# A mixer kernel on one core: the state products of the attention as two 64-column tiles a head

## The chip, the cores and the metric

One core of a Trainium2 chip runs the whole program. The metric is the device time of one execution in microseconds (us), median of three runs. A profile is one execution recorded by the hardware profiler. TensorE (PE, with PEld for its weight loads), VectorE (DVE), ScalarE (ACT), GpSimd (POOL) and SyncE (SP, which here issues DMAs) each run their own list of instructions in order, and semaphores tie the lists together.

## The reference

```
# attention, B,H,S,D = 4,8,768,48
for t in range(S):                      # complex decay a, normalised to |a| <= 0.999
    new_re = ar * S_re - ai * S_im
    new_im = ar * S_im + ai * S_re
    S_re   = new_re + k[t] (outer) v[t]
    y[t]   = q[t] @ S_re
x = y as (B, S, H*D)                    # 4 x 768 x 384
# first MLP block
u = x + ((x^T @ U @ V)^T)               # rank 32 over the sequence
x = u + relu(u @ w1) @ w2               # 384 -> 1536 -> 384
# second MLP block
u = x + real(fft(fft(x, axis=1), axis=2))
x = u + relu(layernorm(u) @ w1') @ w2'
```

## The kernel before

The attention is computed in chunks of 128 time steps: 4 batches of 6 chunks. For each chunk, a chain of DVE, ACT and POOL operations (`decays`, `turns`) turns the decays into factors and multiplies them into queries and keys. The result is `QK` (time on the free axis, 128 partitions); SP copies it by six DMAs to `QT` (96 partitions: 48 real and 48 imaginary parts; 8 heads). Then `products` (written as a generator; one `yield` a step) does on PE:

- `scores` (L501): for each head, keys times queries, 128 x 128, into `sc`; DVE masks it into `pm` (L506).
- `turned` (L511): six transposes of the keys into `kp`; ACT copies them (L513) into `ks`, a tile of 128 time steps x 768 columns, 96 columns a head.
- `summed` for `y` (L522): for each head, `pm` times `v` and, from the second chunk on, `QT` times the state `S`. The stationary operand has 128 columns (time), taken as two tiles of 64 columns (`halves`), which write PSUM partitions 0 to 63 and 64 to 127.
- `summed` for `g` (L522): for each head, `ks` times `v`, which gives what the chunk adds to the state. The stationary operand has 96 columns, taken as a tile of 64 columns and one of 32: the slice is cut at the end of the head.
- DVE then makes the new state `S` of 96 x 384 from `g` (L570, or L572 and L573). There is a `g` in all chunks but the last of a batch: 5 x 4 = 20 state products.

`ks` comes from the pool slots tagged `st` (three of them). The same slots stage the MLP weights, which come in as 64-bit words (`fetch`, L127, tiles `stw`), are turned to f32 by ACT and DVE (L120, L142, L143: `wxw`) and split into a high and a low 16-bit part by ACT (L164) and POOL (L165, L166: `w`). There are 24 such pieces a layer. `check_w` (L176) reads the weights once and writes an unread tile `chk`.

The first MLP's units (`moe_units`) run 12 hidden blocks for each half batch: nine matmuls `hp` of 128 x 384 (L103 to L105), ACT and DVE make `hh` and `hl` from them (L230, L231), and nine matmuls into `acc` (L212, L213, L198). The attention of batch b+1 and, at the end, the Fourier transform of batch 0 are put in beside the units of batch b as side work, some steps a unit. The first batch's attention runs alone, before the first MLP starts (60 to 125 us). The second MLP has the Fourier transforms beside it.

The code gives each step a priority; a list scheduler, run at build time with its own timing of each engine, writes the instruction order of each engine. A change of a few instructions can so move others.

Of the kernel before, what the change touches and what calls it, by code (L numbers as in the profile page):

```python
# [9 lines left out]
BF16 = mybir.dt.bfloat16  # L10
F32 = mybir.dt.float32
F32R = mybir.dt.float32r
I32 = mybir.dt.int32
# [9 lines left out]
DM = H * D  # L23
# [23 lines left out]
def mixer_kernel(ctx, tc, a_in, qk_in, v_in, u_in, v4_in, w_in, cc_in, ss_in, cb_in, sb_in, id_in, mask_in, rows_in, out):  # L47
    nc = tc.nc
    V, A, G, T = nc.vector, nc.scalar, nc.gpsimd, nc.tensor
# [3 lines left out]
    moe = ctx.enter_context(tc.tile_pool(name="moe", bufs=2))  # L53
# [8 lines left out]
    def bank(name, pool=None):  # L62
        pool = pool or pms
        return pool.tile([128, 512], F32, tag={id(pms): "ms", id(pacc): "acc", id(phid): "hid"}[id(pool)], name=name)
# [58 lines left out]

    def fetch(src, name):
        n = src.shape[-1]
        st = moe.tile([128, 384, 2], I32, tag="st", name=f"st{name}", bufs=3)[:, :n]
        nc.sync.dma_start(st.rearrange("p n w -> p (n w)"), src.bitcast(I32))  # L127
        return st

# [41 lines left out]
    def check_w(mi, f, z):  # L171

        hi = wt[mi, f][:, 0, z * 384 : (z + 1) * 384]
        unread = ft(f"chk{mi}_{f}_{z}", [128, 384], BF16, tag="chk", bufs=2)
        at = stats[:, list(BOUNDS).index(("w1", "w2")[z]), mi * FB + f : mi * FB + f + 1]
        V.scalar_tensor_tensor(out=unread, in0=hi, scalar=1.0, in1=hi, op0=ALU.mult, op1=ALU.mult, accum_out=at)  # L176

# [74 lines left out]
    def stat(name, b, c):  # L252
        return stats[:, list(BOUNDS).index(name), b * NC + c : b * NC + c + 1]
# [8 lines left out]
    def attention_pool():  # L262
        pl = attp[0]

        def at(nm, tag=None, bufs=4, shape=(128, 3, 2, 128), dt=F32, pl=pl):
            return pl.tile(list(shape), dt, tag=tag or "t", name=nm, bufs=bufs)

        return at
# [22 lines left out]
    def load_v(b, c):  # L291
        if c == NC:
            b, c = b + 1, 0
        if 0 < b < B:
            t = attention_pool()(f"vin{b}_{c}", "vin", 2, (128, DM))
            nc.sync.dma_start(t, v_in[b, c])
            inp["v", b, c] = t
# [182 lines left out]
    def products(m, j):  # L480

        b, cc = PAIRS[m]
        c = cc[j]
        n = f"{b}_{c}"
        last = c == NC - 1
        at = attention_pool()

        def t3(nm, bufs, shape):
            return at(f"{nm}{n}", nm, bufs, shape)

        QT, QK = qkt[b, c]
        vin = inp["v", b, c]
        sc, pm, kp = [], [], []
        pool = pacc if b == 0 else pms
        halves = slice(0, 64), slice(64, 128)

        def scores(hf):
            ps = bank(f"sc{n}_{hf}").rearrange("p (h t) -> p h t", h=4)
            for h in range(4):
                q = QT[:, hf * 4 + h]  # L500
                T.matmul(ps[:, h, :], q[:, 128:256], q[:, :128], start=True, stop=True)  # L501
            sc.append(ps)

        def masked(hf):
            pm.append(room[:, hf] if b == 0 else at(f"pm{n}_{hf}", "pm", 2, (128, 4, 128)))
            V.tensor_tensor(pm[hf], sc[hf], mask.unsqueeze(1).to_broadcast([128, 4, 128]), ALU.mult)  # L506

        def turned(z):
            kp.append(bank(f"kp{n}_{z}", pool)[:, :384])
            for i in range(3):  # L510
                T.transpose(kp[z][:, i * 128 : (i + 1) * 128], QK[:, z, i, 128:256], ident)  # L511
            src = kp[z].rearrange("t (x h) -> t h x", h=8)
            A.copy(ks.rearrange("t (h z x) -> t h z x", h=8, z=2)[:, :, z, :], src)  # L513

        def summed(out, ops):

            for o, (l, r) in enumerate(ops):
                for h in range(8):
                    hsl = slice(h * 48, (h + 1) * 48)
                    for p in halves:  # L520
                        p = slice(p.start, min(p.stop, l(h).shape[-1]))
                        T.matmul(  # L522
                            out[p, hsl],
                            l(h)[:, p],
                            r[:, hsl],
                            start=h == 0 and o == 0,
                            stop=h == 7 and o == len(ops) - 1,
                            skip_group_check=True,
                        )

        if b == 0:
            if len(rooms) < 4:
                rooms.append(wpl.tile([128, 3, 4, 128], F32, tag="w", name=f"pm{n}"))
            room = rooms[c % 4]
        scores(0)
        scored.append(nc.cur_bb.bb.instructions[-1])
        yield
        scores(1)
        masked(0)
        yield  # L540
        masked(1)
        if not last:
            ks = moe.tile([128, 768], F32, tag="st", name=f"k{n}", bufs=3)
            turned(0)
        yield
        if not last:
            turned(1)
            fe = t3("fe", 2, (96, 8))
            G.tensor_scalar(fe, QT[:, :, 256], 1.0 / FSCALE, 0.0, ALU.mult, ALU.add)
        load_v(b, c + 1)  # L550
        yield
        S = state.get(b)
        yp = bank(f"y{n}", pool)[:, :DM]
        ops = [(lambda h: pm[h // 4][:, h % 4], vin)]
        if S is not None:
            ops.append((lambda h: QT[:, h, :128], S))
        summed(yp, ops)
        yield
        if not last:
            gp = bank(f"g{n}")[:96, :DM]  # L560
            summed(gp, [(lambda h: ks[:, h * 96 : (h + 1) * 96], vin)])
        x = xt[b, c] = xpl[0].tile([128, DM], F32, tag="x", name=f"x{n}", bufs=10)
        A.activation(x, yp, AF.Copy, scale=1.0 / FSCALE)
        yield
        if not last:
            state[b] = sS = t3("S", 2, (96, DM))
            by_head = lambda o: o.rearrange("p (h e) -> p h e", h=8)
            f3 = fe.unsqueeze(2).to_broadcast([96, 8, 48])
            if S is None:
                V.scalar_tensor_tensor(out=by_head(sS), in0=by_head(gp), scalar=FSCALE, in1=f3, op0=ALU.mult, op1=ALU.mult)  # L570
            else:
                V.scalar_tensor_tensor(out=sS, in0=gp, scalar=FSCALE, in1=S, op0=ALU.mult, op1=ALU.add)  # L572
                V.tensor_tensor(by_head(sS), by_head(sS), f3, ALU.mult)  # L573
        yield
        A.activation(yp, x, AF.Square, accum_out=stat("y", b, c))
# [130 lines left out]
    def both(m):  # L706
        return urgent(chain(products(m, 0), products(m, 1)), 250)
# [82 lines left out]
    def ft(name, shape, dt=F32, tag=None, bufs=1):  # L790
        return pfl[0].tile(list(shape), dt, tag=tag or name.split(".")[0], name=name.replace(".", "_"), bufs=bufs)
# [446 lines left out]
```

## Time and profile before

| | us |
|---|---|
| median of 3 runs (lowest, highest) | 987.97 (986.28, 989.13) |
| the profiled execution, its own time | 987.67 |
| its span from first to last instruction | 985.4 |
| PE busy | 865.6 (88%) |
| DVE busy | 612.9 (62%) |
| ACT busy | 410.1 (42%) |
| POOL busy | 243.2 (25%) |

Up to 60 us the inputs come in and PE hardly works. From 60 to 118 us PE does the attention of batch 0, from 165 to 510 us the first MLP with the attention of batches 1 to 3 beside it, from 510 to 600 us the first MLP's last batch with the first Fourier transform and the second layer's weights beside it, and from there to the end the second MLP. A matmul on f32 data stands in the trace as two records, so a product of 16 matmuls has 32 records.

### The profile page before, as it was taken

Reading aid. Unit: us, or ns where it says so; the run is one execution under the profiler, and the core shown is the slowest. Engines: PE = TensorE matmul, PEld = TensorE weight load, DVE = VectorE, ACT = ScalarE, POOL = GpSimd, SP = SyncE. Lnnn points to the kernel's source line nnn. Section 1 sums busy time; section 2 is a strip of 40 time slices with the busy share of each in tenths; the row PEclk is TensorE's granted clock in tenths of the full one; section 3 lists DMA queues with packets and bytes.
Section 4 is the critical chain, followed back from the end, with each engine's and each line's share of the span. In section 5 each row is a group of like instructions: output and inputs, shape, how many; then the busy total and the mean of one; then the engine's idle time right before and its main releaser. Section 6 shows DMA issues by size and latency. Waiting matters only on the chain. (4 is left out here: it accounts for less than half of the span.)

```text
span 985.4 us, 16779 instructions
## 1 busy us (share of the span) xinstructions
PE 865.6 (88%) x6686; PEld 585.0 (59%) x6686; DVE 612.9 (62%) x1116; ACT 410.1 (42%) x767; POOL 243.2 (25%) x271
## 2 busy tenths in 40 slices
PE   0059985799999999999996889999999999999997
PEld 0047843477667676667763455666666765766664
DVE  7976895966776565473389995672645564463221
ACT  8545675667666754542333341122122211322111
POOL 3402453430112012020066551320322232020000
PEclk9999997799999998989999999999999999999999
DMA  9069648557546743514175240110101021000000
GB/s 363 1 83 143 180 129 159 119 100 145 100 121 101 132 105 73 105 34 74 51 228 187 82 121 1 41 41 1 65 18 49 1 81 49 1 25 10 17 25 27
DMA packets 47095, 83.43 MB, mean 85 GB/s; under 512 B 5600, under 2 KB 36064, under 8 KB 47008
## 3 DMA queue, kind: packets, MB, share of 16 engines
q1 hardware_dynamic: 45152, 75.96, 33.3%
q0 software_dynamic: 1856, 6.31, 1.8%
q8 instruction: 54, 0.88, 0.4%
q14 instruction: 33, 0.27, 0.1%
HBM read 53.79 MB, written 9.44 MB: 64 GB/s over the span
## 5 line engine op out<-in xcount | busy, mean ns | idle before, releaser
L231 DVE SCALAR_TENSOR_TENSOR hl<-hp,hh 128x384 f16<-128x384 f32 x192 | 105.6, 551 | 190.9 <-ACT hh L230 190.1
L230 ACT ACTIVATE hh<-hp 128x384 f16<-128x384 f32 x192 | 93.4, 487 | 299.6 <-PE hp L105 285.3
L212 PE MATMUL acc<-w,hh 128*128 128x384 f16 x576 | 190.4, 332 | 8.5 <-ACT hh L230 7.7
L213 PE MATMUL acc<-w,hh 128*128 128x384 f16 x576 | 189.6, 330 | 1.4 <-POOL w L166 1.4
L198 PE MATMUL acc<-w,hl 128*128 128x384 f16 x576 | 127.7, 330 | 0.0
L103 PE MATMUL hp<-u,w 128*128 128x384 f16 x288 | 95.8, 334 | 19.9 <-DVE hl L231 18.8
L105 PE MATMUL hp<-u,w 128*128 128x384 f16 x288 | 96.9, 336 | 3.8 <-POOL w L166 3.8
L104 PE MATMUL hp<-u,w 128*128 128x384 f16 x288 | 96.3, 334 | 1.0 <-DVE u L640 1.0
L103 PE MATMUL hp<-n,w 128*128 128x384 f16 x288 | 93.9, 326 | 1.0 <-DVE hl L231 1.0
L104 PE MATMUL hp<-n,w 128*128 128x384 f16 x288 | 93.9, 326 | 0.0
L105 PE MATMUL hp<-n,w 128*128 128x384 f16 x288 | 93.9, 326 | 0.0
L104 PEld LDWEIGHTS <-w 128*128 128x128 f16 x576 | 56.9, 99 | 60.4 <-issue 26.6
L212 PEld LDWEIGHTS <-hh 128*128 128x128 f16 x576 | 56.9, 99 | 47.8 <-ACT hh L230 11.3
L105 PEld LDWEIGHTS <-w 128*128 128x128 f16 x576 | 56.9, 99 | 43.5 <-POOL w L166 4.2
L198 PEld LDWEIGHTS <-hl 128*128 128x128 f16 x576 | 56.6, 99 | 39.0 <-issue 1.8
L103 PEld LDWEIGHTS <-w 128*128 128x128 f16 x576 | 56.8, 99 | 37.9 <-issue 1.6
L501 PE MATMUL sc<-QT 96*128 96x128 f32 x384 | 59.5, 305 | 20.8 <-DMA QT<-QK 20.5
L213 PEld LDWEIGHTS <-hh 128*128 128x128 f16 x576 | 57.2, 99 | 34.2 <-issue 3.4
L522 PE MATMUL g<-vin,k 128*32 128x48 f32 (+1 forms) x640 | 75.5, 229 | 1.1 <-ACT k L513 1.1
L501 PEld LDWEIGHTS sc<-QT 96*128 96x128 f32 x384 | 53.6, 213 | 24.9 <-issue 20.0
L511 PE MATMUL kp<-ident,QK 128*128 128x128 f32 x120 | 21.0, 297 | 50.5 <-DVE QK L472 50.3
L522 PEld LDWEIGHTS g<-vin,k 128*32 128x32 f32 (+1 forms) x640 | 53.4, 123 | 19.8 <-issue 1.5
(264 smaller groups left out, 1569.3 us busy)
## 6 DMA issues: line engine op xcount, KB each, us to landing
QT<-QK SPq DMA_DIRECT2D x144, 129.0 KB
stw<-in_w_dram SPq DMA_DIRECT2D x48, 384.0 KB
ain<-in_a_dram SPq DMA_DIRECT2D x12, 768.0 KB
qkin<-in_qk_dram SPq DMA_DIRECT2D x12, 768.0 KB
x1d<-x SPq DMA_DIRECT2D x24, 192.0 KB
vin<-in_v_dram SPq DMA_DIRECT2D x18, 192.0 KB
lo<-x1d SPq DMA_DIRECT2D x12, 192.0 KB
out_dram<-lo SPq DMA_DIRECT2D x12, 192.0 KB
```

The source lines that it names most:

```text
L103: T.matmul(o, ah, bh, start=start, stop=False, skip_group_check=skip)
L104: T.matmul(o, ah, bl, start=False, stop=False, skip_group_check=skip)
L105: T.matmul(o, al, bh, start=False, stop=stop, skip_group_check=skip)
L198: T.matmul(acc[t], hl[:, t * 128 : (t + 1) * 128], w2h, start=False, stop=f == FB - 1 and extra is None)
L212: T.matmul(acc[t], hh[:, ts], w2h, start=f == 0, stop=False)
L213: T.matmul(acc[t], hh[:, ts], w2l, start=False, stop=False)
L230: A.activation(hh, hp, AF.Relu)
L231: V.scalar_tensor_tensor(out=hl, in0=hp, scalar=0.0, in1=whole_of(hh), op0=ALU.max, op1=ALU.subtract)
L501: T.matmul(ps[:, h, :], q[:, 128:256], q[:, :128], start=True, stop=True)
L511: T.transpose(kp[z][:, i * 128 : (i + 1) * 128], QK[:, z, i, 128:256], ident)
L522: T.matmul(out[p, hsl], l(h)[:, p], r[:, hsl], start=h == 0 and o == 0, stop=h == 7 and o == len(ops) - 1, skip_group_check=True,)
```

## The change

The keys' tile has 800 columns instead of 768, the last 32 filled with zeros by POOL. Each head's stationary operand for the state product is 128 columns wide, of which the last 32 are the next head's keys (or the zeros), taken as two tiles of 64 columns. The rows 96 to 127 of the product are not read. The slots `st` grow from 3072 to 3200 bytes a partition, and `chk` has one buffer instead of two.

```diff
     def fetch(src, name):
-        st = moe.tile([128, 384, 2], I32, tag="st", name=f"st{name}", bufs=3)[:, :n]
+        st = moe.tile([128, 400, 2], I32, tag="st", name=f"st{name}", bufs=3)[:, :n]
...
     def check_w(mi, f, z):
-        unread = ft(f"chk{mi}_{f}_{z}", [128, 384], BF16, tag="chk", bufs=2)
+        unread = ft(f"chk{mi}_{f}_{z}", [128, 384], BF16, tag="chk", bufs=1)
...
         def turned(z):
-            A.copy(ks.rearrange("t (h z x) -> t h z x", h=8, z=2)[:, :, z, :], src)
+            A.copy(ks[:, :768].rearrange("t (h z x) -> t h z x", h=8, z=2)[:, :, z, :], src)
         def summed(out, ops):
                     for p in halves:
-                        p = slice(p.start, min(p.stop, l(h).shape[-1]))
                         T.matmul(
...
-            ks = moe.tile([128, 768], F32, tag="st", name=f"k{n}", bufs=3)
+            ks = moe.tile([128, 800], F32, tag="st", name=f"k{n}", bufs=3)
+            G.memset(ks[:, 768:], 0.0)
...
-            gp = bank(f"g{n}")[:96, :DM]
-            summed(gp, [(lambda h: ks[:, h * 96 : (h + 1) * 96], vin)])
+            gp = bank(f"g{n}")[:, :DM]
+            summed(gp, [(lambda h: ks[:, h * 96 : h * 96 + 128], vin)])
+            gp = gp[:96]
```

On PE, at the first state product of the program (`g_0` of batch 0; `sc_1` are the next chunk's scores), the order before is:

```order
L501 MATMUL sc_1_1_346<-QT_1_246 128x128 x4
L522 MATMUL g_0_402<-vin_0_126,k_0_305 64x48
L522 MATMUL g_0_402<-vin_0_126,k_0_305 32x48
L522 MATMUL g_0_402<-vin_0_126,k_0_305 64x48
L522 MATMUL g_0_402<-vin_0_126,k_0_305 32x48
L522 MATMUL g_0_402<-vin_0_126,k_0_305 64x48
```

and after the change, where L522 has become L521 and the lines from L562 on are numbered one higher:

```order
L501 MATMUL sc_1_1_347<-QT_1_246 128x128 x4
L521 MATMUL g_0_404<-vin_0_126,k_0_305 64x48 x16
L603 MATMUL z_434<-x_0_421,ust 128x384
L511 MATMUL kp_2_0_484<-ident,QK_2_319 128x128 x3
L511 MATMUL kp_2_1_489<-ident,QK_2_319 128x128 x3
```

The sixteen matmuls that alternated between 64 and 32 rows of output are sixteen of 64. Counted over the whole program's order, the output width changes from one PE matmul to the next 428 times before (306 of them between 64 and 32) and 110 times after (none between 64 and 32).

On DVE, at the end of the attention of batch 3, around the last state (`S_4`) and the first pieces of the second layer's weights (`stw`, `wxw`; `hl` belongs to the first MLP of batch 2), the order before is:

```order
L231 SCALAR_TENSOR_TENSOR hl_2_0_11_4403<-hp_2_0_11_4350,hh_2_0_11_4402 128x384
L120 TENSOR_SCALAR stw_0_1_5055<-stw_0_1_5055 128x384
L143 SCALAR_TENSOR_TENSOR wxw_0_0_5000<-stw_0_0_4998,wxw_0_0_5000 128x384
L640 SCALAR_TENSOR_TENSOR u_1_2_4398<-xp_1_2_4393,u_1_2_4398 128x384
L142 SCALAR_TENSOR_TENSOR wxw_0_1_5057<-wxw_0_1_5057,stw_0_1_5055 128x384
L143 SCALAR_TENSOR_TENSOR wxw_0_1_5057<-stw_0_1_5055,wxw_0_1_5057 128x384
L572 SCALAR_TENSOR_TENSOR S_4_4711<-g_4_4688,S_3_4557 96x384
```

and after:

```order
L143 SCALAR_TENSOR_TENSOR wxw_3_0_5300<-stw_3_0_5298,wxw_3_0_5300 128x384
L120 TENSOR_SCALAR stw_3_1_5350<-stw_3_1_5350 128x384
L142 SCALAR_TENSOR_TENSOR wxw_3_1_5352<-wxw_3_1_5352,stw_3_1_5350 128x384
L143 SCALAR_TENSOR_TENSOR wxw_3_1_5352<-stw_3_1_5350,wxw_3_1_5352 128x384
L120 TENSOR_SCALAR stw_4_0_5398<-stw_4_0_5398 128x384
L142 SCALAR_TENSOR_TENSOR wxw_4_0_5400<-wxw_4_0_5400,stw_4_0_5398 128x384
L143 SCALAR_TENSOR_TENSOR wxw_4_0_5400<-stw_4_0_5398,wxw_4_0_5400 128x384
L120 TENSOR_SCALAR stw_4_1_5454<-stw_4_1_5454 128x384
L573 SCALAR_TENSOR_TENSOR S_4_4731<-g_4_4708,S_3_4576 96x384
```

Before, two pieces of the second layer's weights (0_0 and 0_1) are finished ahead of the last state; after, nine (0_0 to 4_0).

On POOL, while the first layer's weights are made, the order before is:

```order
L394 TENSOR_TENSOR turn_0_436<-ain_0_130,turn_0_436 128x768
L165 TENSOR_SCALAR wxw_0_0_551<-wxw_0_0_551 128x384
L549 TENSOR_SCALAR fe_4_700<-QT_4_393 96x8
L166 TENSOR_TENSOR w_550<-wxw_0_0_551,w_550 128x384
L165 TENSOR_SCALAR wxw_0_1_561<-wxw_0_1_561 128x384
```

and after:

```order
L394 TENSOR_TENSOR turn_0_438<-ain_0_130,turn_0_438 128x768
L543 MEMSET k_3_589 128x32
L165 TENSOR_SCALAR wxw_0_0_554<-wxw_0_0_554 128x384
L549 TENSOR_SCALAR fe_4_705<-QT_4_395 96x8
L166 TENSOR_TENSOR w_553<-wxw_0_0_554,w_553 128x384
```

A fill of zeros stands in POOL's list ahead of each chunk's state product, 20 in all; it has to wait until the slot's last reader is done (for the third and later chunks of batch 0, an earlier state product on PE).

## Rows read from the trace of the kernel before

**Rows 1.** The page's busy time, share of the span and instructions, by engine.
```profile
PE 865.6 (88%) x6686; PEld 585.0 (59%) x6686; DVE 612.9 (62%) x1116; ACT 410.1 (42%) x767; POOL 243.2 (25%) x271
```
**Rows 2.** Windows: length, busy PE, PEld, DVE, ACT, POOL (records), PE clock, DMA.
```profile
60.00:118.00 58.00, 55.20 (x672) 46.04 (x673) 43.65 (x69) 29.80 (x56) 14.61 (x17) 0.97 0.80 144
...
165.00:260.00 95.00, 88.08 (x855) 63.65 (x855) 73.59 (x109) 63.25 (x111) 28.36 (x25) 0.91 0.53 112
260.00:330.00 70.00, 66.86 (x574) 46.14 (x572) 46.49 (x69) 50.23 (x87) 12.81 (x8) 1.00 0.63 115
330.00:420.00 90.00, 87.25 (x725) 61.03 (x726) 51.98 (x73) 51.44 (x90) 13.03 (x9) 0.94 0.53 99
420.00:510.00 90.00, 89.28 (x839) 62.81 (x838) 50.36 (x85) 31.63 (x61) 16.02 (x21) 0.96 0.31 76
510.00:600.00 90.00, 70.11 (x409) 42.33 (x408) 86.51 (x198) 32.38 (x71) 50.74 (x55) 0.96 0.42 136
600.00:985.00 385.00, 375.72 (x2422) 242.28 (x2420) 175.70 (x399) 80.36 (x172) 63.83 (x88) 1.00 0.09 29
```
**Rows 3.** Timeline of PE, 99 to 105 us: start, duration, what, records.
```profile
99.11 1.14 PE L522 MATMUL y<-vin,pm 128*64 128x48 f32 x32
100.08 1.10 PE L522 MATMUL y<-S,QT 96*64 96x48 f32 x32
101.02 3.62 PE L522 MATMUL g<-vin,k 128*64 128x48 f32 x32
104.56 0.71 PE L501 MATMUL sc<-QT 96*128 96x128 f32 x4
```
**Rows 4.** Timeline of PE, 304 to 305 us, where both products are interleaved.
```profile
304.68 0.27 PE L522 MATMUL g<-vin,k 128*32 128x48 f32 x2
304.88 0.26 PE L522 MATMUL y<-S,QT 96*64 96x48 f32 x1
...
304.98 0.22 PE L522 MATMUL y<-S,QT 96*64 96x48 f32 x1
304.98 0.22 PE L522 MATMUL g<-vin,k 128*64 128x48 f32 x1
305.04 0.28 PE L522 MATMUL y<-S,QT 96*64 96x48 f32 x2
305.25 0.27 PE L522 MATMUL g<-vin,k 128*32 128x48 f32 x2
```
**Rows 5.** Groups by form, PE's weight loads: busy us, mean ns | idle before.
```profile
L522 PEld LDWEIGHTS g<-vin,k 128*64 128x64 f32 x320 | 31.1, 137 | 11.0 <-issue 1.5 <-ACT k L513 1.4 <-ACT turn L459 0.6
...
L522 PEld LDWEIGHTS y<-S,QT 96*64 96x64 f32 x640 | 25.4, 141 | 3.3 <-issue 1.1
L522 PEld LDWEIGHTS g<-vin,k 128*32 128x32 f32 x320 | 22.2, 109 | 8.8
```
**Rows 6.** Windows of PE's two half-clock stretches, columns as in Rows 2.
```profile
366.00:376.00 10.00, 10.00 (x56) 6.88 (x55) 4.83 (x6) 4.13 (x9) 2.06 (x2) 0.51 0.26 54
...
431.00:438.00 7.00, 7.00 (x35) 4.04 (x35) 6.75 (x9) 1.43 (x3) 3.97 (x2) 0.51 0.10 29
```
**Rows 7.** Waits of PE, 165 to 510 us: us in total, times, longest.
```profile
PE sc L501 <- DMA QT<-QK: 10.2, 2, 9.9
PE acc L212 <- ACT hh L230: 5.1, 7, 1.5
PE hp L105 <- POOL w L166: 3.8, 1, 3.8
```
**Rows 8.** Groups by form, DVE work on a weight piece: busy us, mean ns | idle.
```profile
L143 DVE SCALAR_TENSOR_TENSOR wxw<-stw,wxw 128x384 int32<-128x384 int32 x48 | 33.5, 704 | 0.2
...
L142 DVE SCALAR_TENSOR_TENSOR wxw<-wxw,stw 128x384 int32<-128x384 int32 x48 | 31.0, 653 | 2.2 <-ACT wxw L120 2.0
...
L120 DVE TENSOR_SCALAR stw<-stw 128x384 int32<-128x384 int32 x48 | 24.3, 505 | 15.9 <-DMA stw<-in_w_dram 15.9
```
**Rows 9.** Groups by form, a fill of zeros on POOL.
```profile
L814 POOL MEMSET ee<- 128x4 f32 x4 | 0.5, 121 | 10.1 <-DVE eel L848 10.1
```

## The prediction

> **What bounds the kernel.** First the busy times: PE is busy 88% of the span, DVE 62%, POOL 25% [rows 1]. That is an average over stages, so next the windows [rows 2]. From 165 to 260, 260 to 330, 330 to 420 and 420 to 510 us PE is busy 93, 96, 97 and 99%; there a microsecond less on PE is a microsecond off the end, as long as the others keep up. From 60 to 118 us PE is busy 95%, but what follows it waits for something else (below). From 510 to 600 us DVE is the bound: 86.5 of 90 us, with PE idle 19.9. From 600 us on PE is the bound again, and the change has nothing there: its 385 us stay.
>
> The timeline of PE shows what a state product costs [rows 3]. The output product with `pm` starts at 99.11 and its successor at 100.08: 0.97 us for 32 records. The one with `S` takes 0.94 us (100.08 to 101.02), and the state product, again 32 records, on as many columns of `v`, takes 3.54 us (101.02 to 104.56). The durations of single records do not show this, since matmuls overlap; the starts do. Where both products are interleaved, the reason is seen [rows 4]: five groups of 64-wide matmuls start within 0.16 us (304.88 to 305.04), whichever tile they write, but the 32-wide one behind them starts 0.21 us later, and the 64-wide one behind a 32-wide one 0.20 us later (304.68 to 304.88). So it is the step from one width to the other that costs, some 0.15 us beyond the 0.06 between two `y` matmuls (0.97 us for 16). A state product has 8 x 2 steps, 16 x 0.15 = 2.4 us, and 0.97 + 2.4 is near the 3.54 measured.
>
> The Trainium skill has this as a rule (TensorEngine Tiling (Array Packing), Key Properties): a change of the tiling mode, other than a change of the tile, drains the engine. The trace agrees, with the 0.2 us above.
>
> **The change part by part.** *State products.* All 16 matmuls of a product are 64 wide, so no step is left inside it; I take it to run like the `y` products, 0.95 us instead of 3.54, 2.6 us less. There are 20. Five are in the attention of batch 0, 15 beside the first MLP: 13 us and 39 us. Of the 428 changes of width in the order, 306 are these. The matmuls that are widened cost nothing in themselves, as a `y` tile of 64 starts every 0.06 us. Their weight loads get longer, 109 to 137 ns in the mean [rows 5], but the `y` product's loads of 141 ns also run within 0.94 us for 32, so they overlap; if that were wrong, see the third rival.
>
> *15 products beside the first MLP.* PE is the bound there, so the 39 us come off, less new waits. In 165 to 260 us, DVE has 73.6 us of work in 95 us [rows 2]. Five of the 15 products fall in it, so the stretch would shrink to some 80 us and DVE would be busy 92% of it. Where DVE is busy 96% (510 to 600 us), PE idles 22%; 22% of 80 us is 17 us, the upper bound; the lower is nothing. I take 7, nearer to the row with DVE at 77%, where PE now idles 6.9. In 330 to 510 us, DVE would go from 57% to some 67%; PE now idles 3.5 us in 180, and I add 3 (bounds 0 and 8, twice the idle time of the first stretch's share). New waits: 10 us, between 0 and 25.
>
> *Clock.* In two stretches the granted clock is at half, the lower of the two levels of 1.2 and 2.4 GHz: 366 to 376 and 431 to 438 us [rows 6]. PE is busy throughout both and just before them, and what ran ahead of each, or in it, is a state product. The 0.91 of 165 to 260 us [rows 2] means another 17 us at half; I put 7 of them to a state product, as an estimate, and the rest to PE's waits there. If the array idles inside such a product, as the starts say, the fall follows from that and would go with it. Half of 10 + 7 + 7 us is 12 us at most; new waits can bring other falls. I take 6, between 0 and 12.
>
> *Batch 0's five products, 60 to 118 us.* The 13 us are at once up against waits that are not PE's work. The next batch's scores wait 9.9 us for `QT` at about 165 us [rows 7], at the end of a chain on ACT, DVE and SP that starts when batch 0's attention is done, and that runs beside the weight pieces. It is earlier by what batch 0's chain (keys, DMA, state) gains, and of its links only the state products are faster. Bounds 0 and 13; I take 4, a third, since the chunks' own `QT` copies and DVE (43.7 of 58 us) [rows 2] run at nearly PE's pace.
>
> *Weight pieces moved.* Ahead of the last state, DVE's list now has nine pieces instead of two. A piece is 0.70 + 0.65 + 0.51 = 1.86 us of DVE [rows 8], so 13 us of DVE's work leave the stretch of 510 to 600 us, where DVE is the bound and PE idles 19.9. That is a gain of 13 at most. Against it, every piece waits for its DMA in DVE's list, and `hl`, for which PE waits, and the last state stand behind it. DVE waited 15.9 us for all 48 pieces' DMAs [rows 8]; if half of that fell on these, it would cost 8, which I take as the bound. On SP, four pieces' DMAs now stand ahead of the load of the last chunk's `v`, which the last `y` needs; a piece that waits for its slot holds that too, within the same 8. I take a gain of 2.
>
> *Fill, slots, `chk`.* A fill is 0.12 us [rows 9], 2.4 us for 20 on an engine that is busy 25%. What is queued behind it on POOL are the weights' low parts (L165, L166), and for these PE waits 3.8 us once [rows 7]. Each fill waits for the slot that ACT's copy of the keys waits for anyway. I put it at 0, bounds 0 and 5, within the new waits above. The wider slots move no more bytes by DMA. `chk` is written by DVE alone, in order, so one buffer adds no wait on another engine: 0.
>
> *Sum.* 39 - 10 + 6 + 4 + 2 + 0 = 41 us. From the profiled execution's own 987.67 us that leaves 946.7; the median of the runs shown is 987.97, 0.3 higher, so the forecast is 946 to 947, and I say 946.
>
> **The rivals.** *The others take more of it.* DVE becomes the bound in the stretches beside the first MLP, new waits 25 us, clock 3, batch 0 and the pieces 0: 39 - 25 + 3 = 17, 971 us (960 to 982). For it: DVE at 92% in 165 to 260 us, and DVE and ACT hold the chain to the next `QT`. Against it: DVE itself waits for PE there, which would get shorter, and PE's waits from 165 to 510 us that lie with ACT and POOL are 5 and 4 us [rows 7].
>
> *It gives more.* The waits stay small (4), the clock gives 9, batch 0 gives 9, the pieces 7: 39 - 4 + 9 + 9 + 7 = 60, 928 us. For it: batch 0's PE is busy 95%, and the weights' slots are freed by the state products.
>
> *Weight loads set the pace (slower).* A product's loads add up to 16 x 137 + 16 x 109 ns = 3.9 us [rows 5], close to the 3.54 measured. If they ran one after the other in the state product, 32 of 137 ns would be 4.4 us, 0.45 more, and 20 x 0.45 = 9 us slower: 997 us. It decides from the point where a load can't overlap the matmul ahead of it. Against it: in the `y` products, 32 loads of 141 ns would be 4.5 us, and they take 0.94. The Trainium skill says that a load's time goes by its columns, at 1.2 per ns (TensorE: Matmul & The Clock Gate, LDWEIGHTS). An estimate by that page is 27 ns more for each of 320 loads, 8.5 us; the rows' 28 ns agree.
>
> *It doesn't do what it says.* The product is slow for a reason that stays, such as its writing to one bank from two tiles, or another engine holds every stretch: 988 us, no change. Against it: the `y` products also write one bank from two tiles.
>
> **How the numbers follow.** Forecast 0.70, with a range of its own of 932 to 960; more absorbed 0.17; more gain 0.06; weight loads 0.04; no change 0.03. The range of 928 to 970 takes in the forecast's, half of the first rival and the second's centre. Less than 0.3% either way, 3 us, can't be told from no change. Faster 0.70 + 0.17 + 0.06 = 0.93; same 0.03; slower 0.04.
>
> **What would show it.** The state products' starts: right if the next matmul starts about 0.95 us after the product's first, wrong at over 2. The half-clock stretches behind state products should be gone. PE's idle time between the first scores of batch 1 and the end of batch 3's attention, now 13.5 us (345 less the busy times of 165 to 510 us), should be 18 to 30; much more would mean the first rival, and then DVE's busy share there is over 85%. The wait for batch 1's `QT` should still be there, of 5 us or more. From the first matmul of the second MLP to the end nothing should differ by more than 2 us. The forecast is wrong if the product is short and the time still over 970.

## The result, and the profile after

The changed kernel takes 979.1 us (median of 4, 977.09 to 979.26) against 988.5 for the kernel before in the same comparison: a ratio of 0.9904, interval 0.9883 to 0.9925. It is faster, but by some 9 us in place of the 41 forecast, and outside the range of 928 to 970. The profiled execution took 977.09 us, its span 975.2. Ratios, here and below, leave out executions that took over 1.5% longer than the fastest of the same kernel, so they and not the medians are compared.

The first view is the page's busy times, as [rows 1]: 39.9 us of PE's work are gone (865.6 before), the other engines have what they had.
```profile
PE 825.7 (85%) x6686; PEld 560.2 (57%) x6686; DVE 613.0 (63%) x1116; ACT 408.5 (42%) x767; POOL 246.5 (25%) x291
```
The timeline of PE around 102 us answers to [rows 3].
```profile
100.22 1.14 PE L521 MATMUL y<-vin,pm 128*64 128x48 f32 x32
101.19 1.10 PE L521 MATMUL y<-S,QT 96*64 96x48 f32 x32
102.13 1.10 PE L521 MATMUL g<-vin,k 128*64 128x48 f32 x32
103.16 1.05 PE L501 MATMUL sc<-QT 96*128 96x128 f32 x7
```
The state product is followed after 1.03 us (102.13 to 103.16), 3.54 before. So the product itself does what was forecast, and the question is where its time went. The windows, with the columns of [rows 2]:
```profile
60.00:118.00 58.00, 48.40 (x686) 43.06 (x687) 45.82 (x70) 30.47 (x59) 17.76 (x20) 0.88 0.78 152
...
165.00:260.00 95.00, 76.59 (x848) 55.45 (x848) 72.97 (x108) 59.44 (x105) 30.02 (x30) 0.90 0.49 105
260.00:330.00 70.00, 64.25 (x588) 43.76 (x587) 47.52 (x70) 49.76 (x86) 12.56 (x11) 0.96 0.60 118
330.00:420.00 90.00, 83.66 (x751) 58.23 (x749) 54.36 (x76) 55.02 (x97) 13.05 (x12) 0.96 0.54 99
420.00:510.00 90.00, 82.51 (x831) 58.17 (x829) 57.90 (x107) 38.17 (x79) 24.87 (x33) 0.92 0.48 127
510.00:600.00 90.00, 71.27 (x442) 44.66 (x440) 74.67 (x175) 25.44 (x53) 39.40 (x43) 0.98 0.26 86
```
From 165 to 510 us PE now idles 18.4 + 5.8 + 6.3 + 7.5 = 38.0 us, 13.5 before. DVE isn't full there (73.0 of 95 us from 165 to 260 us). Of the waits from 165 to 510 us (us in total, times, longest) none is large, and they lie mostly with ACT, POOL and DVE. The five largest:
```profile
PE g L521 <- ACT k L513: 7.2, 5, 3.4
PE hp L105 <- POOL w L166: 6.5, 2, 5.8
PE acc L212 <- ACT hh L230: 6.4, 7, 3.0
PE y L521 <- DVE pm L506: 3.6, 4, 1.8
PE sc L501 <- DVE S L573: 2.5, 2, 1.9
```
The long wait for `QT` of [rows 7] is still there, 8.9 us for 9.9, but now ends at 162.6 us, ahead of this stretch.

Where the gain comes and goes is seen from when each half batch of the first MLP starts (the first matmul of `hp`, from the timelines of PE; "old order" is run 5 below and "pieces held" run 6). Each column is one execution, so a difference of a few us is not more than a hint:

| half batch | before | changed | gain | old order | gain | pieces held | gain |
|---|---|---|---|---|---|---|---|
| batch 0, first | 125.1 | 123.3 | 1.8 | 124.9 | 0.2 | 123.7 | 1.3 |
| batch 0, second | 211.2 | 211.8 | -0.6 | 209.7 | 1.5 | 212.1 | -0.9 |
| batch 1, first | 280.9 | 285.8 | -4.9 | 277.6 | 3.3 | 287.4 | -6.4 |
| batch 2, first | 425.2 | 417.9 | 7.3 | 411.3 | 13.9 | 420.4 | 4.8 |
| batch 2, second | 499.5 | 484.1 | 15.5 | 474.7 | 24.8 | 479.5 | 20.0 |
| batch 3, first | 562.4 | 558.6 | 3.9 | 538.8 | 23.7 | 535.0 | 27.4 |
| second MLP | 655.8 | 645.7 | 10.2 | 630.5 | 25.3 | 633.1 | 22.8 |

Two things stand out in the changed kernel. Up to batch 1's first half nothing is gained though ten of the 20 products are done; and 11.6 us that had been gained by 484 us are given back by 559, of which 6.3 return by the start of the second MLP. In that stretch PE waits for `hl`, on DVE. The waits of PE from 500 to 565 us, before and after:
```profile
PE hp L103 <- DVE hl L231: 8.3, 5, 3.8
```
```profile
PE hp L103 <- DVE hl L231: 18.1, 9, 4.8
```
The longest of the nine, on the timeline of all engines of the changed kernel (start, duration, what, and in brackets the idle time before it and its releaser):
```profile
521.31 1.09 POOL L811 DMA_INDIRECT hi<-x1d,rows  x1 [0.16 <-issue]
...
521.78 5.69 DVE L176 SCALAR_TENSOR_TENSOR chk<-w 128x384 bf16<-128x384 f16 x1
...
522.42 1.79 POOL L166 TENSOR_TENSOR w<-wxw,w 128x384 f16<-128x384 f32 x2
...
526.06 0.98 POOL L834 TENSOR_TENSOR ye<-x,x 128x384 f32<-128x384 f32 x1
...
527.99 0.55 DVE L231 SCALAR_TENSOR_TENSOR hl<-hp,hh 128x384 f16<-128x384 f32 x1
...
528.60 0.48 PE L103 MATMUL hp<-u,w 128*128 128x384 f16 x1 [4.77 <-DVE hl L231]
```
A sum for the range test (`chk`), 0.54 to 0.56 us in most of the 48 places, took 5.69 us while POOL was busy from 521.3 to 527.0 without a gap, and `hl` stood behind it in DVE's list. It is not what sets the two lists apart: in run 5 below, which has the old lists, such a sum took 4.52 us.

### The profile page after: what moved, and what is told of

It reads as the page before. It is cut to its first block, busy times and chain, and to the rows that moved or that the text cites. A ratio compares the mean times of both kernels' runs of the same rounds, so it can differ in the third digit from the quotient of the medians.

```text
span 975.2 us, 16821 instructions
## 1 busy us (share of the span) xinstructions
PE 825.7 (85%) x6686; PEld 560.2 (57%) x6686; DVE 613.0 (63%) x1116; ACT 408.5 (42%) x767; POOL 246.5 (25%) x291
## 5 line engine op out<-in xcount | busy, mean ns | idle before, releaser
L501 PE MATMUL sc<-QT 96*128 96x128 f32 x384 | 61.9, 313 | 30.0 <-DMA QT<-QK 23.4
L165 POOL TENSOR_SCALAR wxw<-wxw 128x384 f32<-128x384 f32 x48 | 32.5, 676 | 80.8 <-ACT w L164 80.0
L166 POOL TENSOR_TENSOR w<-wxw,w 128x384 f16<-128x384 f32 x48 | 51.2, 1069 | 2.9
```

Source lines behind the costliest of these rows:

```text
L165: G.tensor_scalar(x, x, WP[z], 0.0, ALU.mult, ALU.add)
L166: G.tensor_tensor(w[:, 1, zs], x, w[:, 0, zs], ALU.subtract)
```

## The experiments

Theories at the start. A: the elementwise work of a pair of chunks sets the pace from 172 to 346 us, and time taken off PE turns into waits. B: the new order of the lists loses it. C: the clock falls in the new waits. To tell the widths from the order, most kernels hold every engine's list to a recorded one:
```diff
+        for blob in ORDERS.values():
...
+            for p, q in zip(at, at[1:]):
...
+                tc.add_manual_dep(
+                    traced[q],
+                    traced[p].name,
...
+                    reason="pinned",
+                )
```
Here `at` is one engine's list, as places in the traced program. This queues each instruction behind the one before it and adds no wait. (Line numbers in these kernels are 9 to 23 higher than in the kernel before, at the places named here.) Runs 8 to 10 and 13 to 16 leave out loads, sums or weights that the reference needs, and serve for the time alone. Ratios are to the kernel before, run on the same chip, with 95% intervals; its own median there was 990.6 to 994.2 us.

| run | products | order | us | ratio |
|---|---|---|---|---|
| 1 widths alone | wide | old | 968.3 | 0.9784 (0.9733 to 0.9835) |
| 2 all but the widths | narrow | new | 998.1 | 1.0080 (1.0039 to 1.0120) |
| 3 no range sums | wide | new | 973.5 | 0.9849 (0.9792 to 0.9907) |
| 4 no range sums | narrow | old | 990.2 | 0.9995 (0.9959 to 1.0032) |
| 5 whole change | wide | old | 964.5 | 0.9735 (0.9687 to 0.9782) |
| 6 pieces held | wide | new, one line | 966.8 | 0.9748 (0.9701 to 0.9794) |
| 7 L394 ahead of `fe` | wide | old | 971.8 | 0.9806 (0.9759 to 0.9853) |
| 8 and no reload | wide | old | 960.6 | 0.9687 (0.9640 to 0.9735) |
| 9 and no range sums | wide | old | 953.7 | 0.9596 (0.9555 to 0.9638) |
| 10 as 9 | narrow | old | 984.7 | 0.9896 (0.9846 to 0.9945) |
| 11 late batches only | 10 wide | old | 974.1 | 0.9822 (0.9774 to 0.9869) |
| 12 one switch a product | grouped | old | 976.2 | 0.9836 (0.9793 to 0.9880) |
| 13 half the pieces | wide | old | 954.6 | 0.9639 (0.9604 to 0.9673) |
| 14 half the pieces | narrow | old | 977.7 | 0.9877 (0.9827 to 0.9927) |
| 15 as 13 and 9 | wide | old | 939.1 | 0.9484 (0.9449 to 0.9520) |
| 16 as 14 and 10 | narrow | old | 970.0 | 0.9780 (0.9743 to 0.9818) |

### Order or widths (runs 1, 2, 5, 6)

Run 1: the last head keeps 64 and 32 columns, the others get 64 and 64.
```diff
-            gp = bank(f"g{n}")[:96, :DM]
-            summed(gp, [(lambda h: ks[:, h * 96 : (h + 1) * 96], vin)])
+            gp = bank(f"g{n}")[:, :DM]
+            summed(gp, [(lambda h: ks[:, h * 96 : min(h * 96 + 128, 768)], vin)])
+            gp = gp[:96]
```


> Kernel before with the state products alone widened (second tile of heads 0 to 6 is 64 columns, of head 7 it stays 32; no wider tile, no fill), and the order of every engine's instructions held to that of the kernel before. Theory A (the elementwise work of a pair of chunks paces 172 to 346 us, so time taken off the PE turns into waits there): 975 to 981 us, as the changed kernel. Rival B (the new order of the lists, with the fill on POOL, loses what the narrow tiles gave back): 950 us or less. Rival C (the clock falls in new waits and eats the gain): 965 to 975, with more half-clock stretches than before.

Run 2: the change with its products narrow again, in the changed kernel's order.
```diff
+                        p = slice(p.start, min(p.stop, l(h).shape[-1]))
...
-            gp = bank(f"g{n}")[:, :DM]
-            summed(gp, [(lambda h: ks[:, h * 96 : h * 96 + 128], vin)])
-            gp = gp[:96]
+            gp = bank(f"g{n}")[:96, :DM]
+            summed(gp, [(lambda h: ks[:, h * 96 : (h + 1) * 96], vin)])
```


> Changed kernel with the state products as before it (64 and 32 columns), all else of it kept: the 800-column tile, the fill on POOL, the single check buffer, and the order of every engine's instructions held to that of the changed kernel. Theory A: the new order by itself costs little, 985 to 993 us, since the product's 52 us of PE time lie for the most part in PE waits. Rival B: over 1000 us, the order loses 15 us or more by itself, and the widths bring 25 or more in it.

Run 1, at 968, lay between theories A and B, and run 2, at 998, between A's 985 to 993 and B's 1000. Together: the widths are worth 21 us in the old order and 17 in the new one (1.0080 - 0.9904), and the new order by itself costs 8 us with narrow products and 12 with wide ones (17 against run 5, which differs from the changed kernel in the lists alone). So neither A nor B alone. The 968 is also in C's range, but C's mark is hardly there: from 165 to 510 us the stretches at half clock add up to some 38 us in run 1 and 35 in the kernel before, worth 2 us at most.

Run 5 is the whole change, the order of the kernel before held:
```diff
-            G.memset(ks[:, 768:], 0.0)
+            FREE.add(G.memset(ks[:, 768:], 0.0).ins.name)
```
(`FREE` names what is not held.)

> All edits of the change (two 64-column tiles, 800-column tile, fill on POOL, single check buffer), but with the order of every engine's instructions held to that of the kernel before; the 20 fills alone stand where the scheduler puts them. If it is the new order that loses (some 9 us at 484 to 600, where pieces of the second MLP's weights stand earlier in DVE's list): 965 to 971 us, ratio 0.976 to 0.981, as with the narrower edit of the first run. If the fill or the single check buffer loses it: 975 us or more.

Slightly better than expected, 964.5. The fill and the single `chk` buffer cost nothing that shows. Its page and its windows, with the columns of [rows 1] and [rows 2]:
```profile
PE 816.7 (85%) x6686; PEld 551.9 (57%) x6686; DVE 616.1 (64%) x1116; ACT 408.3 (43%) x767; POOL 252.6 (26%) x291
```
```profile
165.00:260.00 95.00, 78.65 (x864) 55.06 (x864) 75.20 (x110) 63.11 (x112) 28.38 (x31) 0.92 0.52 111
260.00:330.00 70.00, 63.26 (x599) 43.45 (x598) 46.46 (x69) 51.20 (x88) 12.39 (x11) 0.98 0.65 116
330.00:420.00 90.00, 83.24 (x829) 59.02 (x828) 57.99 (x82) 54.46 (x95) 17.47 (x13) 0.96 0.50 97
420.00:510.00 90.00, 83.02 (x795) 57.09 (x794) 63.70 (x130) 32.37 (x68) 31.77 (x38) 1.00 0.51 146
```
Run 6 is the changed kernel with one line, which keeps the second MLP's pieces from being issued ahead of batch 3:
```diff
                 side = Side(dft(0), 14, 30)
+                anchor()
```


> Changed kernel with one line more: the second MLP's weight pieces may not be issued on DVE and ACT ahead of what is in their lists when the last first-MLP batch is written. Order otherwise the scheduler's own. If the pieces ahead cost the 9 us that the changed kernel gives back at 484 to 600: 966 to 972 us. If the cause there is the order of PE's own list or POOL: 976 to 981 us.

966.8, as expected: the line is worth some 15 us (0.9904 to 0.9748, intervals apart). Its waits for `hl` from 500 to 565 us are the shortest of all:
```profile
PE hp L103 <- DVE hl L231: 4.2, 4, 2.0
```
and the same stage in four kernels, from the start of batch 2's second half to that of batch 3's first, shows what that does to PE (before, changed, run 5, run 6):
```profile
499.50:562.40 62.90, 49.01 (x325) 29.09 (x322) 61.37 (x140) 20.91 (x45) 39.80 (x46) 0.97 0.52 173
```
```profile
484.10:558.60 74.50, 55.64 (x428) 34.94 (x427) 66.48 (x142) 26.88 (x58) 45.94 (x53) 0.95 0.52 167
```
```profile
474.70:538.80 64.10, 49.48 (x326) 29.06 (x324) 62.86 (x142) 21.92 (x47) 41.91 (x46) 0.97 0.51 170
```
```profile
479.50:535.00 55.50, 52.40 (x433) 34.40 (x432) 37.82 (x97) 12.76 (x28) 18.99 (x24) 1.00 0.35 118
```
PE idles 13.9, 18.9, 14.6 and 3.1 us in it. DVE is 98% busy there before the change and in run 5, 89% in the changed kernel, 68% in run 6. The pieces come later and take back some of it: the gain is 27.4 us at batch 3 and 22.8 at the second MLP in the table above. Run 6 does more than undo the move: DVE finishes its first piece at 536.7 us, in the kernel before at 490.1. Runs 5 and 6 beat both kernels.

### The loops of the pairs (runs 3, 4, 7 to 10)

The scan of the phases (L438), one for each pair, comes every 31 to 35 us. The changed kernel's, from the timeline of DVE:
```profile
214.24 1.75 DVE L438 TENSOR_TENSOR_SCAN turn<-going,turn 128x768 f32<-128x768 uint8 x1
...
249.17 1.75 DVE L438 TENSOR_TENSOR_SCAN turn<-going,turn 128x768 f32<-128x768 uint8 x1
...
280.74 1.75 DVE L438 TENSOR_TENSOR_SCAN turn<-going,turn 128x768 f32<-128x768 uint8 x1
...
312.40 1.75 DVE L438 TENSOR_TENSOR_SCAN turn<-going,turn 128x768 f32<-128x768 uint8 x1
```
The kernel before has them at 214.77, 248.72, 281.26 and 312.96: 11.5 us of PE's work less in 165 to 260 us (76.6 for 88.1) has not moved them. Followed back from a wait of PE, one link of the chain is this (timeline of all engines of the changed kernel):
```profile
262.25 5.98 SPq L476 DMA_DIRECT2D QT<-QK  x9
...
269.16 0.90 POOL L549 TENSOR_SCALAR fe<-QT 96x8 f32<-96x8 f32 x1 [16.55 <-DMA QT<-QK]
270.02 1.81 POOL L394 TENSOR_TENSOR turn<-ain,turn 128x768 f32<-128x768 f32 x1
...
271.86 0.33 SPq L280 DMA_DIRECT2D ain<-in_a_dram  x1
...
276.83 0.84 ACT L362 ACTIVATE ls<-ain 128x768 f32<-128x768 f32 x1 [1.65 <-DMA ain<-in_a_dram]
...
278.40 0.47 ACT L230 ACTIVATE hh<-hp 128x384 f16<-128x384 f32 x1
...
278.93 0.50 PE L212 MATMUL acc<-w,hh 128*128 128x384 f16 x1 [2.95 <-ACT hh L230]
```
`hh`, which PE needs, stands in ACT's list behind the next pair's squares; these wait for the reload of the only `a` buffer, and that for POOL's L394, which stands behind a copy that waits for `QT`. Three edits cut links of it. Runs 3 and 4 leave out two sums on ACT:
```diff
+                    if b == 0:
                         A.activation(unused, re, AF.Relu, bias=least, ..., accum_out=stat("im", b, cc[0]))
+                    if b == 0:
                         A.activation(unused, s2_, AF.Relu, bias=most, accum_out=stat("im", b, cc[1]))
```


> Changed kernel, order held, without the two range sums of batches 1 to 3 (ACT lines 368 and 369, 2.3 us of ACT a pair, which only guard the range of the input). Theory A: each of the pairs 4 to 11 comes round 2 to 3 us sooner (33.4 us now), the first MLP starts batch 2 some 8 us and the whole ends 10 to 20 us sooner: 959 to 969 us. Rivals B and C: what ACT does beside the PE costs nothing, 975 to 980 us.

> Kernel before, order held, without the same two range sums. Theory A: the PE had little idle time left there (7 of 95 us at 165 to 260, 3 of 70 at 260 to 330), so 3 to 8 us at most: 980 to 986 us, and the change is worth 15 us or more between this kernel and the one without the sums after it. If the pairs' work bounds both kernels alike: 10 us or more here too, 975 or less. Rivals B and C: 986 to 989 us.

Theory A missed in both. Run 3 took 973.5, 5 us less than the change with intervals that overlap, and its scans stayed (214.3, 248.3, 280.0, 311.3); run 4 did nothing, as rivals B and C had it. Run 7 moves L394 ahead of `fe` in POOL's list (no line of the program changes), and run 8 also ends the reloads:
```diff
+        if kind == "a" and m >= 5:
+            inp[kind, m] = inp[kind, 4]
+            return
```


> The widths in the old order (first run), with one swap in POOL's list for pairs 6 to 11: the product that reads the a input (line 394) stands ahead of the copy of the state's decay (fe, line 549), which waits there for a QT transfer. Theory A, refined: the loop that paces pairs is QK, QT's transfers, fe on POOL, line 394, the reload of the single a buffer, ACT 362, DVE's scan, QK (31 to 34 us a pair). Then a pair gets 2 to 4 us shorter from 214 us on and the whole 4 to 12 us: 956 to 964 us. If the PE is held by something else there: 966 to 970 us.

> As the run before it (swap in POOL's list), and the a input is not loaded again after pair 4: pairs 5 to 11 read pair 4's (7 loads of 768 KB left out, output not the reference's). Theory A, refined: the reload and its wait leave the loop, pairs 4 to 6 us shorter (28 to 30 us apart), the whole 946 to 960 us. If the loop is not what holds the PE at 125 to 354 us: 964 to 970 us, and the pairs as far apart as before.

Run 7 brought nothing (971.8): L394 came 2 us sooner and the scans where they were (212.5, 247.9, 280.9, 313.5). Run 8 came to the end of what was expected, 960.6, but its first three scans stand still as well (214.5, 248.1, 281.1); the fourth comes at 310.3, 3 us sooner than in run 1 (313.3). That a second chain, ACT's and DVE's over the single `turn` buffer, is as long, so that two loops lie side by side, was read from its trace and is not shown here. Runs 9 and 10 cut both:

> The run without reloads (wide products, old order, line 394 ahead of fe, no reload of a after pair 4) and also without the two range sums on ACT (lines 368 and 369). Output not the reference's. Theory A, twice refined: two loops of equal length (33 us) hold a pair, one by QT's transfers and the reload of a, one by ACT's and DVE's chain over the single turn buffer; each cut alone moved pairs little because the other stayed. With both cut pairs are 29 to 31 us apart from 214 us on, and the whole is 942 to 953 us (ratio 0.952 to 0.963). If neither holds the PE: as the run without reloads, 957 to 963 us (0.966 to 0.971), pairs still 33 us apart.

> The same cuts on the kernel before, state products narrow. Theory A: with 2.6 us more of PE a product the PE is the bound here, so cutting the pairs' loops gives 0 to 6 us: 982 to 990 us (ratio 0.992 to 1.0), and the change is worth 33 us or more between this kernel and the wide one with the same cuts, against 21 to 26 us with the loops whole. If the loops hold the narrow kernel as well: 975 us or less, and the change is worth no more than before.

Run 9's scans, from the timeline of DVE:
```profile
211.11 1.75 DVE L453 TENSOR_TENSOR_SCAN turn<-going,turn 128x768 f32<-128x768 uint8 x1
...
246.18 1.75 DVE L453 TENSOR_TENSOR_SCAN turn<-going,turn 128x768 f32<-128x768 uint8 x1
...
277.91 1.75 DVE L453 TENSOR_TENSOR_SCAN turn<-going,turn 128x768 f32<-128x768 uint8 x1
...
306.06 1.75 DVE L453 TENSOR_TENSOR_SCAN turn<-going,turn 128x768 f32<-128x768 uint8 x1
```
The last two are 31.7 and 28.2 us apart, the next two scans (339.6 and 370.1) 33.6 and 30.4. From 211 us on the mean is 31.8 us, 33.8 in run 1: less was gained than the 29 to 31 expected, and the time of 953.7 is at the end of what was expected. Run 10, 984.7, is inside theory A's time, and its scans stay 32 to 35 us apart with PE 98 to 99% busy from 260 to 510 us, as that theory has it. But it gained 7 to 10 us where 0 to 6 had been expected; where, is not shown, since its profiled execution, 989.6, is the slowest of its six. The change is worth 0.9896 - 0.9596, or 30 us, between these two, where 33 or more had been expected. The same edit with whole loops, run 1, is worth 21.

### Early products, pieces, and the switch (runs 11 to 16)

Run 11 widens only the products of batches 2 and 3:
```diff
+            summed(gp, [(lambda h: ks[:, h * 96 : min(h * 96 + (128 if b > 1 else 96), 768)], vin)])
```


> Kernel before, order held, with only the state products of batches 2 and 3 wide (10 of 20, 26 us of PE time less). Theory A: the products of batches 0 and 1 lie beside pairs that set the pace, so these 10 bring nearly all that the 20 did in this order (0.9735 to 0.978): 0.976 to 0.984, some 966 to 974 us. If each product is worth the same: half, ratio 0.987 to 0.989, 977 to 980 us.

974.1, as expected: these ten bring 18 us, so the ten early ones bring 4 of the 21 of run 1, or 9 of the 26 of run 5, give or take 7. Runs 13 to 16 then leave out half of the first MLP's weight pieces, for which PE waits at 181 us:
```diff
+KEEP = 6
...
+            if parts16[0] and f >= KEEP:
...
+                    wt[mi, f] = wboth[f - KEEP][:, mi]
+                yield
+                continue
```


> Wide products, old order (first run), with half of the first MLP's weights left out: blocks 6 to 11 use the weights of blocks 0 to 5 (12 of 24 pieces, output not the reference's). Theory W (the pieces, done at 200 us, hold 118 to 212 us): batch 0's second half starts at 203 us or sooner in place of 210 to 212, and the whole is 948 to 960 us (ratio 0.958 to 0.970). If the pairs alone hold that stretch: 208 us or later, 962 to 968 us.

> The same half of the pieces left out, products narrow. Theory W: here the products' 13 us of PE time in that stretch come up as soon as the pieces don't hold it, so it gains less than the wide one: 0 to 7 us, 981 to 988 us, ratio 0.993 to 1.0, and the change is worth 28 us or more between the two (22 to 26 with all pieces). If pieces hold both alike: as much gain as the wide one, and the change is worth the same 22 to 26.

> Wide products with half of the pieces and with both loops of the pairs cut (no reload of a after pair 4, no range sums, line 394 ahead of fe). Theories W and A together: what held the PE beside its own work is eased in both stretches, 934 to 946 us (ratio 0.945 to 0.957). If there is a third thing that holds it: 948 us or more.

> The same on narrow products. Theories W and A together: the PE's own work bounds it, 974 to 984 us, and the change is worth 35 us or more between this kernel and the wide one (30 with all the pieces). If the change is worth no more than 30 here, its lost half is not in what these cuts ease.

Theory W was right on the place: batch 0's second half starts at 196.6 us in run 13 (207.6 to 212.1 in the wide kernels with all pieces), and run 15 is the fastest, 939.1. It was wrong on the change: with fewer pieces the narrow kernel gains about as much (12 us, the wide one 14 from run 1; its second half starts at 196.4 us in run 14), and the change is worth 24 us between runs 14 and 13 and 29 between 16 and 15, where 28 and 35 had been expected. Run 16, 970.0, is faster than the 974 to 984 expected.

Run 12 keeps the narrow tiles and does a product's eight 64-column tiles before its eight 32-column ones:
```diff
-                for h in range(8):
...
-                    for p in halves:
...
+                tiles = [(h, p) for h in range(8) for p in halves]
+                for h, p in sorted(tiles, key=lambda x: x[1].start) if grouped else tiles:
```


> Kernel before, order held, tiles as before (64 and 32 columns), but each state product does its eight 64-column tiles first and then its eight 32-column ones: one change of width inside a product in place of 15. If the change of width is what a narrow tile cost (0.17 us each, 15 a product): a product takes 1.1 to 1.4 us and the whole is 964 to 972 us, with no wider tile and no fill. If the 32-column tiles themselves are slow: a product stays over 2.5 us and the whole at 980 us or more.

```profile
465.99 1.89 PE L532 MATMUL g<-vin,k 128*64 128x48 f32 x32
467.82 0.90 PE L532 MATMUL y<-S,QT 96*64 96x48 f32 x22
```
A product takes 1.83 us (to the next start): between the two cases expected, and the whole, 976.2, as well. So at least 1.7 of the 2.6 us were the changes of width. The other 0.8 us are not the 32 columns as such. In this product's records the eight 64-column tiles, now all on the same columns of the array, start 58 ns apart, 0.93 us for 16 records; in the `y` product behind it, whose tiles alternate between two halves, two records start every 58 ns. The 32-column tiles start 42 ns apart, and the two changes of width, into them and out of them, take 0.15 and 0.14 us from start to start.

## Why the forecast was wrong

In the terms of the sum, 39 - 10 + 6 + 4 + 2, and by the profiles of the kernel before, of run 5 (the whole change, old lists) and of the changed kernel: from 165 us to the start of batch 2's second half, run 5's PE is busy 41.1 us less (279.9 from 321.0) for the 39 and the clock's 6, and idles 16.3 us more (29.8 from 13.5) for the 10; batch 0 gives 0.2 for the 4. The windows of that stretch in the three kernels (before, run 5, changed), with the columns of [rows 2]:
```profile
165.00:499.50 334.50, 320.97 (x2882) 226.91 (x2882) 212.24 (x313) 192.90 (x339) 62.70 (x49) 0.95 0.49 97
```
```profile
165.00:474.70 309.70, 279.86 (x2874) 197.84 (x2874) 209.16 (x312) 189.13 (x334) 64.36 (x62) 0.96 0.52 103
```
```profile
165.00:484.10 319.10, 281.85 (x2759) 198.22 (x2759) 211.36 (x314) 188.83 (x334) 67.03 (x67) 0.93 0.51 103
```
Run 5 is left with 25.3 us at the second MLP. The new lists then take 15.1 of it (10.2 left) where the sum had 2 to be gained. These are single executions; by the ratios it is 26 us and 17.

*State products, 2.6 us less each.* Right: 1.03 us from a product to its successor, 0.95 forecast. PE's busy time fell by 39.9 us in the changed kernel and by 48.9 in run 5 (865.6 to 816.7), near 20 x 2.5; the mean granted clock of the execution was 0.972 before, 0.971 in run 5 and 0.960 in the changed kernel. That the step from one width to the other was the price is borne out for 1.7 of the 2.6 us at least (run 12).

*Weight pieces moved, "I take a gain of 2".* This step failed most. Of the new lists the sum priced the moved pieces alone, and the rest at nothing, without a reason. The new lists cost 17 us (run 5 and the changed kernel, the same program but for the lists: 0.9735 and 0.9904, intervals apart), outside the bounds of -8 to 13. Against the pieces it counted only the waits for their DMAs; PE's waits for `hl` from 500 to 565 us went from 8.3 to 18.1 us. With the pieces held the change takes 966.8, inside the range, 15 us less. How much the move from two pieces to nine costs by itself stays open: run 6 holds them back further than the kernel before did, and 6.6 of the 15.1 us between the profiles of run 5 and of the changed kernel are missing at the start of batch 2 (13.9 - 7.3), at 418 us, ahead of the second layer's first load at 454.3. What in the lists loses those is not shown.

*"New waits: 10 us, between 0 and 25."* The mechanism was named and the size was off: 16.3 us more in the old lists, within the bounds, and 23.7 (37.2 from 13.5) in the changed kernel up to the same point. The reasoning by DVE's busy share missed it, since DVE idled too: the waits of 165 to 510 us lie with ACT, POOL and DVE. The first rival had the size right (971), but not the reason; its mark, DVE over 85% busy, is not met (77%).

*Clock, +6.* Right in the old lists, wrong in the new ones. From 165 to 510 us the stretches at half clock add up to 35 us before (twice the missing share of each window), to 25 in run 5, a gain of up to 5 us, and to 46 (19 + 6 + 7 + 14) in the changed kernel, a loss of up to 5.5. In run 5, PE is busy throughout from 420 to 475 us at full clock, where the kernel before fell to half at 431 behind a narrow product. In the changed kernel the clock fell at 354, 432 and 470 us, and ahead of each PE had idled: 5.1 us from 340 to 354, 2.3 from 422 to 432, 2.4 from 460 to 470. So theory C holds for the changed kernel, and is small.

*Batch 0, +4.* The first MLP starts 1.8 us sooner, and in the old order 0.2. Beside the wait for `QT`, which stayed as forecast (8.9 us, 9.9 before), the clock of 60 to 118 us takes part. It was 0.82 to 0.88 in the ten kernels with wide products in every batch. In the seven with narrow ones in batch 0 it was 0.88 to 1.00, and 0.97 in the profile compared with here. Among kernels with the old lists and a clock of 0.88 there, the narrow ones (runs 4 and 16) start the first MLP at 129.5 and 130.8 us, the wide ones (runs 1, 7 and 13) at 126.5, 123.9 and 124.9. So at about the same clock the products of batch 0 gave 3 to 7 us, which the comparison with this profile of the kernel before hides. That the wide products bring the lower clock is not shown: three narrow kernels have 0.88 too.

*Fill and slots, 0; second MLP unchanged.* Right: run 5, and a gain that stays at 10.1 to 10.3 us from 646 us on.

*What stays open.* In a held order 21 to 26 us of the 52 come off. From the table, old order: 0.2 of the 13 of batch 0's products, 3.1 of batch 1's, 10.6 of batch 2's, 9.8 of batch 3's, with the clock's part above in the first. The pieces were shown to hold the place where the early ones vanish, but cutting them speeds the narrow kernel nearly as much (12 us, 14). Cutting the two loops brings the wide kernel 19 us and the narrow one 10, so the change is worth 30 in place of 21 (29 with fewer pieces as well): the loops account for some 8 us of what does not come off, a difference that only just clears its intervals. What hides the rest is not shown. Theory A is borne out to that extent only.

## What to carry to other kernels

Where a scheduler writes the lists, price the new list apart from the edit: the same edit was worth 9 us in the order that came with it and 26 in the old one, and one line that held the moved work back gave most of that back. An engine that is busy 93 to 99% need not yield its time one for one when the other engines' lists hold waits as well: look at what returns at a fixed interval (here a scan every 33 us, which 11.5 us less of PE's work did not move). Compare executions at the same granted clock before a few us are put to an edit. And where narrow and wide tiles alternate on PE, try one width: here a product went from 3.54 to 1.03 us.

## What was not expected of the hardware

DVE can be held up beside POOL, by much: a sum of 0.56 us took 5.69, as shown above, and in run 8 a scan that takes 1.75 us alone took 3.25 beside POOL's product with the `a` input, which had started first (timeline of both engines):
```profile
267.88 1.86 POOL L407 TENSOR_TENSOR turn<-ain,turn 128x768 f32<-128x768 f32 x1 [16.45 <-ACT turn L109]
...
268.10 3.25 DVE L409 TENSOR_TENSOR_SCAN ls<-starts,ls 128x768 f32<-128x768 uint8 x1
```
It is not always DVE that waits: at 545.9 us of the changed kernel a `chk` sum took its 0.54 us in the midst of POOL's L834, which took 2.19 us and at 526.1 us 0.98. The Trainium skill has a rule for it (SBUF — State Buffer, SBUF: two separate sides): the two engines share a pair of ports, which one instruction holds to its end while the other waits. The durations agree in kind; that one DVE instruction lasted through six POOL ones, an indirect DMA's issue among them, is more than the Trainium skill tells.

Tiles of one width that use the same columns of the array one after the other take twice as long as tiles that alternate between two halves: in run 12 the 64-column tiles of the state product start one record every 58 ns, those of the `y` product behind it two. The rule of the Trainium skill that different tiles load and multiply side by side (TensorEngine Tiling (Array Packing), Key Properties) agrees.
